# Score stores on ScalarE's queue, a later second batch and later value loads in a fused attention and expert kernel

## The chip, the cores and the metric

The kernel runs on one core of a Trainium2 chip. A core has five engines that work at the same time, each through its own instructions in order: TensorE (PE in the profile, with its weight loads as PEld), VectorE (DVE), ScalarE (ACT), GpSimd (POOL) and SyncE (SP). They meet at semaphores. Transfers between the chip's main memory (HBM) and the core's own memory (SBUF) are made by 16 DMA engines; an engine's instruction only starts one. Matrix products land in a small memory of eight banks (PSUM).

The metric is the device time of one execution in microseconds, lower being better.

## The reference

Eight batches of talking-heads attention with 12 heads, 448 positions and 64 dimensions a head, followed by a gated feed-forward network on all 3584 tokens:

```python
scores = scale * np.matmul(q, k.transpose(0, 1, 3, 2))
scores = np.einsum('bhij,hg->bgij', scores, w_pre)
scores = scores - np.max(scores, axis=-1, keepdims=True)
attn = np.exp(scores)
attn = attn / (np.sum(attn, axis=-1, keepdims=True) + 1e-09)
attn = np.einsum('bhij,hg->bgij', attn, w_post)
attn_out = np.matmul(attn, v)
x = attn_out.transpose(0, 2, 1, 3).reshape(B * S, H * D)
out = ((x @ w1) * (x @ w2) @ w3) @ w_out
```

The two einsums mix the twelve heads with each other, one before and one after the softmax. That is why the scores of all heads of a query row must be together before the softmax of that row can begin.

## The kernel before

**Scores and their way through memory.** `qk` (L166) computes one score unit (b, p, c): batch b, head pair p of six, and a block c of 128 query rows (c = 0, 1, 2; the fourth block, c = 3, holds the last 64 rows of two head pairs). It takes two PSUM banks, eight matmuls, and two copies into a tile `st` of 128 x 2 x 448 floats (L179 and L180, both on ACT but for the first block of batch 0). The tile is then stored to `raw_d[b]` in HBM, where a row holds all heads side by side. A unit with c < 3 is one store of 448 KB (L188); one with c = 3 is two of 224 KB (L185). There are 21 units a batch.

`st` has two buffers in each of two pools: units of batch 0 with an odd p use `qp`, all others use `kp`. The first block of batch 0 goes to a tile `sz` of its own; its first 48 rows (FIRST) are stored at once, and the other 80 a little later in one transfer of 1680 KB, called `held` (L805, made at L881).

**The loop.** Everything after the start runs in a loop over n (L889), called steps here. There are 45 tiles of ten query rows in a batch; a pair m of tiles takes two steps. In an even step n = 2m, `fetch(m + 2)` loads the raw scores of a tile pair from HBM into one of two `r` buffers (L202), DVE finds the row minima (`largest`, L227) and ACT the exponentials (`exp`, L235). In an odd step DVE and POOL scale the post-mixing weights (L244 to L247), `post` multiplies them in (L260, PE), ACT copies that out (L274), and `mix(m + 1)` does the pre-mixing of the next pair (L220, PE). A block of 15 tiles is later multiplied with the values (`av`, L301, PE); for batch 0 the first of these products stand at steps 19 and 21.

**Which unit runs in which step** is set by a table `qks` (L809 to L819). Batch 0's units with c = 1, 2 take steps 0 to 11 and those with c = 3 steps 12 to 14. Batch 1's 21 units begin at step 11 and come every 28/21 steps; later batches are spread over 45 steps each. A unit with c = 0 has its queries and keys (`kq`, 448 KB, L157) loaded six steps ahead. Values (`v`, 256 KB, L286) are loaded one per step from step 6 to 11 for batch 0, and one by one after that.

**The order on SP.** Before the change every transfer is issued by SP. A step issues in this order: the fetch, then whatever the step before left in the list `later` (the stores of that step's score units among it), then the remaining `kq` columns of batch 0 or one value load, then the `kq` loads of the table, then one piece of weights (`cs`, L103, 384 KB). So a store is issued in the step after its copies, behind that step's fetch.

**What else runs meanwhile.** The weights come as 64-bit words, and in nearly every step of the opening one piece is converted to float32: ACT squares (L110), DVE puts the bits together (L121 to L124), ACT and POOL split the result in two parts (L129, L130). w3 and w_out are folded into one matrix on PE (L360); from step 18 on this folding is spread over the steps by `shares` (L833) so that PE is evenly full.

Of the kernel before, what the change touches and what calls it, by code (L numbers as in the profile page):

```python
# [17 lines left out]
HP = H // 2  # L18
IB = 10
GI = H * IB  # L20
NB = -(-S // IB)
QT, NJ = 128, 4
# [5 lines left out]
PP = 64  # L28
JB = S // PP
SETS = NB * B // 2  # L30
FIRST = 48
# [19 lines left out]
class Kernel:  # L51
# [114 lines left out]
    def qk(self, b, p, c, banks):  # L166


        nc = self.nc
        ps = [self.bank(i, f"psq{b}_{p}_{c}_{s}")[:, :S] for s, i in enumerate(banks)]  # L170
        for z, (t, q, k) in enumerate(self.parts(b, p, c)):
            for s in range(2):
                rows = slice(s * D, (s + 1) * D)
                nc.tensor.matmul(ps[s][z * PP:(z + 1) * PP], t[rows, q:q + PP], t[rows, k:k + S], start=True, stop=True)  # L174
        if b == c == 0:
            st = self.sz[:, 2 * p:2 * p + 2]
        else:
            st = (self.qp if b == 0 and p % 2 else self.kp).tile([128, 2, S], F32, tag="st", name=f"st{b}_{p}_{c}", bufs=2)
        nc.scalar.copy(st[:, 0], ps[0])  # L179
        (nc.vector.tensor_copy if b == c == 0 else nc.scalar.copy)(st[:, 1], ps[1])  # L180
        raw = self.raw_d[b]
        if c == 3:
            def store():
                for z in range(2):
                    nc.sync.dma_start(raw[3 * QT:, 2 * (p + z) - 2:2 * (p + z)], st[z * PP:(z + 1) * PP])  # L185
            return store
        n = QT if b or c else FIRST
        return lambda: nc.sync.dma_start(raw[c * QT:c * QT + n, 2 * p:2 * p + 2], st[:n])  # L188

# [549 lines left out]
    def run(self):  # L741
        nc, tc = self.nc, self.tc
# [52 lines left out]
        held = []  # L795
# [6 lines left out]
        next(fold_pieces)  # L802
        for f in held:
            f()
        held = lambda: nc.sync.dma_start(self.raw_d[0][FIRST:QT], self.sz[FIRST:])  # L805

# [1 line left out]
        for n, u in enumerate([(0, p, c) for c in (1, 2) for p in range(HP)] + [(0, p, 3) for p in range(1, HP, 2)]):  # L810
            qks[n] = [u]
        for b in range(1, B):
            first, per = (11, 28 / 21) if b == 1 else ((b - 1) * NB - 6, NB / 21)
            units = [(b, p, c) for g in range(0, HP, 2) for p, c in [*itertools.product((g, g + 1), range(3)), (g + 1, 3)]]
            for i, (b, p, c) in enumerate(units):
                n = int(first + i * per) | (b > 1)
                qks.setdefault(n, []).append((b, p, c))
                if c == 0:
                    loads.setdefault(max(n - 6, 0), []).append((b, p))  # L819
        for b in range(B):  # L820
            for a in range(NG):
                for g in range(HP):
                    n = (b * NB + (a + 1) * GB + 3) | 1
# [25 lines left out]
        for pair in range(ONE // 2, B // 2 - 1):  # L849
            first = P_AT if pair == ONE // 2 else 2 * NB * (pair + 1) + 13  # L850
# [5 lines left out]
        def advance(count):  # L856
            nonlocal done
            for _ in range(min(count, total - done)):
                next(background)
                done += 1  # L860
                self.age += len(self.ends) > 0
                if self.age > 2:
                    self.do_ends()

        def there(p):

            f, r = divmod(p - 3 - 2 * KF, 3)
            return 2 * KF * 3 * (1 + f) + (0, 9, 18)[r] if f >= 0 else min(max(3 * (p - 3), 0), KF * 3)
# [3 lines left out]
        def others(p):  # L872
            nc.sync.dma_start(self.kqs[0, p][:, QT + S:], self.kq0[p][:, QT + S:])
# [4 lines left out]
            self.fetch(m)  # L878
        next(fold_pieces)
        next(fold_pieces)  # L880
        held()  # L881
        next(fold_pieces)
        next(fold_pieces)
        self.mix(0)
# [4 lines left out]
        for n in range(N + 6):  # L889
            self.step, third = n, False  # L890
            if n == GB + 1:
                self.close("qp")
                self.xp = [self.pool("xp0", 1)]
            if n == SWITCH:
                assert done == total
                next(background, None)
                self.do_ends()
                self.do_soon()
                self.do_later()
                assert not fold_pieces  # L900
                self.close("fp")
                self.wp = self.pool("wp", 5, side="right")
                self.up = self.pool("up", 1, side="right")
                self.xp.append(self.pool("xp1", 1, side="right"))
                background, total, done = self.experts(phases), (E_1 + E_2) * ONE + P_1 * (B - ONE) // 2, 0
            if n == LATE:
                assert done >= E_1
                self.close("xp0", "cx")
                self.xq, self.cb = self.pool("xq", 2), self.pool("cb", 1)
            if n == PAIR:  # L910

                assert done >= 2 * E_1 + E_2 and unit_pieces is None and not self.jobs and not self.ys
                self.do_ends()
                self.do_soon()
                self.do_later()
                self.pairs, self.w_ahead = True, 4
                self.close("xp1", "cb", "xq", "cs")
                self.xq = self.pool("xq", 2)
                self.up2 = self.pool("up2", 1, side="right")
                self.free += range(N_UP, NS)  # L920
                setup = self.pair_setup(phases)
            if PAIR <= n < PAIR + 7:
                next(setup, None)
            m, odd = divmod(n, 2)
            if not odd and LF <= n + LF < N:
                self.fetch(m + LF // 2)
            self.do_later()
            if n + 3 < HP:
                others(n + 3)
            elif HP <= n < 2 * HP:  # L930
                self.load_v()
            for x in loads.get(n, []):
                self.load_kq(*x)

            p, pieces = self.n_made - 1 if fold_pieces else 2 * KF + 3 * KF, None
            if avs.get(n):
                pass
            elif fold_pieces:
                f = (self.n_made - 1 - 2 * KF) // 3
                if f < 2 or done >= 2 * KF * 3 * (f - 1):  # L940
                    pieces = fold_pieces
                    if next(pieces, self) is self:
                        fold_pieces = pieces = None
            if m < SETS:
                if odd:
                    self.scale(m)
                else:
                    self.largest(m)
            self.do_soon()
            if pieces:  # L950
                next(pieces)
            elif unit_pieces and not fold_pieces and not avs.get(n):
                ahead = 1 if n < SWITCH else 2 * done // (3 * K1) + 4 + (done > 0)
                if n_pieces < ahead:
                    n_pieces += 1
                    if next(unit_pieces, self) is self:
                        unit_pieces = None
                    else:
                        next(unit_pieces)
                        third = True  # L960
            now = share.get(n, 0)
            if n < SWITCH:

                wanted += now
                now = max(min(there(p), KF * 3 + wanted) - done, 0)
            self.do_sums()

            advance(now // 2)
            self.do_ends()
            if not odd and m < SETS:  # L970
                self.exp(m)
            advance(now - now // 2)
            for x in avs.get(n, []):
                self.av(*x)
            self.do_ends()
            if odd and 1 <= m <= SETS:
                self.post(m - 1)
            if odd and m + 1 < SETS:
                self.mix(m + 1)
            self.do_ends()  # L980
            for i, x in enumerate(qks.get(n, [])):
                self.later.append(self.qk(*x, (6, 7) if i else (0, 1)))
            if third:
                next(unit_pieces)

# [66 lines left out]
```

## Time and profile before

| | |
|---|---|
| median of 3 runs | 1444.0 us (1441.49 to 1446.57) |
| the profiled execution | 1437.83 us |
| its span, first to last instruction | 1436.1 us |
| mean granted TensorE clock | 0.986 |
| PE busy | 1382.4 us, 96% of the span |
| ACT busy | 832.4 us, 58% |
| DVE busy | 741.1 us, 52% |
| moved by the DMA engines | 416.87 MB, mean 290 GB/s |

All of it goes through one hardware queue, SP's:

```profile
q1 hardware_dynamic: 203552, 413.94, 87.6%
```

The columns are packets, megabytes, and the share of the 16 DMA engines' span that the packets took. Times within the profile are of the profiled execution, in microseconds from its start. In the views, `out<-in` names what an instruction writes and reads, `xN` counts merged instructions, and brackets at the end of a row of the timeline give how long the engine was idle before it and what ended that wait. A DMA row on SP (SPq) is only the issue; the data lands later.

### The profile page before, as it was taken

What the parts mean: (1) busy time and instruction counts of PE and PEld (TensorE: products, weight loads), DVE (VectorE), ACT (ScalarE), POOL (GpSimd) and SP (SyncE); (2) the same over time, 40 slices, a digit from 0 to 9 for tenths busy, and PEclk for the clock granted to TensorE, in tenths of its full rate; (3) what the DMA queues carried; (4) which work ended last, traced back from release to release, by engine and by line L of the source; (5) the groups of instructions that cost most, each with busy time, mean ns of one, the idle gap of its engine ahead of it and who ended that gap; (6) DMA issues with size and microseconds to landing.
All of it is one profiled execution on the core that took longest, in us unless ns stands there. A gap on an engine that the chain in (4) does not pass through costs nothing.

```text
span 1436.1 us, 45775 instructions
## 1 busy us (share of the span) xinstructions
PE 1382.4 (96%) x18684; PEld 1055.2 (73%) x18684; DVE 741.1 (52%) x1497; ACT 832.4 (58%) x1952; POOL 620.3 (43%) x754
## 2 busy tenths in 40 slices
PE   5889999999999999999999999999999999999998
PEld 2457786776677667776777777777777777899988
DVE  6867566767544544432444436334444446345563
ACT  4867666777766666665656556556555445422231
POOL 2433233434433544532345336334335446446693
PEclk7989999999999999999999999999999999999999
DMA  8998789999999999999989979799879757698775
GB/s 294 366 326 279 236 270 322 320 312 317 324 286 348 355 356 330 362 346 349 287 275 290 320 259 280 249 323 354 288 229 281 241 177 223 195 337 270 231 232 171
DMA packets 203761, 416.87 MB, mean 290 GB/s; under 512 B 20528, under 2 KB 120112, under 8 KB 203472
## 3 DMA queue, kind: packets, MB, share of 16 engines
q1 hardware_dynamic: 203552, 413.94, 87.6%
q8 instruction: 149, 2.44, 0.7%
q14 instruction: 60, 0.49, 0.1%
HBM read 279.77 MB, written 134.09 MB: 288 GB/s over the span
## 4 chain that ended last, share of the span: by engine, by line
PE 82%; DMA 8%; DVE 4%; ACT 2%; issue 1%; POOL 1%; SPq 0%; DVEq 0%; POOLq 0%; ACTq 0%
PE e L702 21%; PE psa L301 11%; PE pso L260 10%; PE psm L220 9%; PE psq L174 7%; PE eg L522 5%; PE psf L360 4%; PE eo L553 4%; PE e2o L702 4%; PE e1o L702 4%; PE e3o L702 4%; DMA wu<-w_d 3%; DMA r<-raw_d 2%; DMA raw_d<-st 2%; ACT e L235 1%
## 5 line engine op out<-in xcount | busy, mean ns | idle before, releaser
L247 POOL TENSOR_SCALAR w<-wpo,ri 128x60 f32<-128x60 f32 x360 | 180.7, 518 | 485.1 <-DVE ri L245 465.3
L227 DVE TENSOR_REDUCE mn<-psm 128x1 f32<-128x448 f32 x360 | 207.7, 618 | 321.6 <-PE psm L220 321.3
L274 ACT COPY mt<-pso 128x480 f32<-128x480 f32 x352 | 197.9, 621 | 185.8 <-PE pso L260 185.6
L702 PE MATMUL e<-eh,wu 128*128 128x448 f32 x1008 | 296.8, 371 | 6.4 <-DVE c L656 3.2
L235 ACT ACTIVATE e<-psm,mn 128x448 f32<-128x448 f32 x360 | 226.8, 643 | 7.9 <-DVE mn L227 7.9
L702 PEld LDWEIGHTS e<-eh,wu 128*128 128x128 f32 x1008 | 187.5, 188 | 52.2 <-issue 26.8
L260 PEld LDWEIGHTS pso<-w,e 60*64 60x64 f32 x10080 | 175.2, 135 | 51.0 <-issue 42.5
L220 PE MATMUL psm<-r,wsc 60*64 60x448 f32 (+1 forms) x1440 | 191.2, 550 | 19.1 <-DVE cx L124 8.3
L260 PE MATMUL pso<-w,e 60*64 60x60 f32 x10080 | 199.1, 224 | 0.4 <-ACT mt L274 0.3
L702 PE MATMUL e<-el,wu 128*128 128x448 f32 x504 | 186.9, 371 | 0.0
L301 PE MATMUL psa<-mt,v 128*64 128x150 f32 (+1 forms) x2304 | 156.9, 292 | 4.1 <-ACT st L179 4.1
L301 PEld LDWEIGHTS psa<-mt,v 128*64 128x64 f32 x2304 | 143.6, 137 | 20.1 <-ACT st L179 6.7
L174 PE MATMUL psq<-kq 64*64 64x448 f32 x1176 | 154.6, 542 | 2.4 <-ACT st L179 2.4
L656 DVE TENSOR_TENSOR c<-c,e 128x448 f32<-128x448 f32 x168 | 101.7, 618 | 87.7 <-PE e L702 82.9
L179 ACT COPY st<-psq 128x448 f32<-128x448 f32 x162 | 86.4, 533 | 73.7 <-ACT mt L274 34.1
L522 PE MATMUL eg<-xh,wu 128*128 128x448 f32 x384 | 119.2, 381 | 6.3 <-DMA wu<-w_d 6.3
L641 POOL TENSOR_TENSOR el<-x,eh 128x448 fp32r<-128x448 f32 x90 | 103.7, 1170 | 32.8 <-ACT eh L640 29.9
L702 PEld LDWEIGHTS e<-el,wu 128*128 128x128 f32 x504 | 94.6, 188 | 22.5 <-issue 14.1
L174 PEld LDWEIGHTS psq<-kq 64*64 64x64 f32 x1176 | 60.8, 135 | 56.4 <-issue 28.8
L522 PEld LDWEIGHTS eg<-xh,wu 128*128 128x128 f32 x384 | 71.9, 190 | 38.7 <-issue 24.0
L244 DVE TENSOR_SCALAR sa<-sm 128x2 f32<-128x2 f32 x180 | 34.9, 194 | 113.6 <-ACT e L235 113.1
L180 ACT COPY st<-psq 128x448 f32<-128x448 f32 x162 | 87.6, 541 | 0.0
(99 smaller groups left out, 2010.1 us busy)
## 6 DMA issues: line engine op xcount, KB each, us to landing
r<-raw_d SPq DMA_DIRECT2D x344, 210.0 KB, 5.1
raw_d<-st SPq DMA_DIRECT2D x138, 448.0 KB, 6.1
wu<-w_d SPq DMA_DIRECT2D x104, 384.0 KB, 6.7
wu<-s_d SPq DMA_DIRECT2D x96, 384.0 KB, 4.8
wu<-w_d SPq DMA_DIRECT2D x51, 512.0 KB, 5.5
kq<-kq SPq DMA_DIRECT2D x42, 448.0 KB, 7.0
wu<-s_d SPq DMA_DIRECT2D x36, 512.0 KB, 4.9
x<-x_d SPq DMA_DIRECT2D x72, 224.0 KB, 5.7
```

The lines of the kernel that those rows point to most:

```text
L174: nc.tensor.matmul(ps[s][z * PP:(z + 1) * PP], t[rows, q:q + PP], t[rows, k:k + S], start=True, stop=True)
L220: nc.tensor.matmul(ps[s][c * PP:(c + 1) * PP, :S], self.wsc[k], r[k, c], start=True, stop=True)
L227: self.nc.vector.tensor_reduce(mn[:, s:s + 1], self.psm[m][s][:, :S], axis=AX.X, op=ALU.min)
L235: nc.scalar.activation(e, p[:, :S], AF.Exp, bias=mn[:, s:s + 1], scale=-1.0, accum_out=sm[:, s:s + 1])
L247: nc.gpsimd.tensor_scalar_mul(w2[:, s], self.wpo, ri[:, s:s + 1])
L260: nc.tensor.matmul(self.pso[c][z * PP:(z + 1) * PP, at:at + HK], e[k, j * PP:(j + 1) * PP], w2s[k, s], start=True, stop=True)
L274: self.nc.scalar.copy(dst.rearrange("p j g (s i) -> p j s g i", s=2), src)
L301: nc.tensor.matmul(self.psa[rows, g % 3, :W], v[:, j, rows], mt[:, j, 2 * g + s, :W], start=(j == 0), stop=(j == NJ - 1))
L522: nc.tensor.matmul(p, u[:, k % (K1 // 2), x], xs[y][:, k], start=(k == 0 and t == 0), stop=(k == K1 - 1 and t == 2))
L641: nc.gpsimd.tensor_tensor(lo, x, hi.bitcast(F32), op=ALU.subtract)
L656: nc.vector.tensor_tensor(a[out], a[to[0]], p, op=ALU.add)
L702: nc.tensor.matmul(p, w[:, k, x], ops[m, k][y], start=(k == 0 and t == 0), stop=(k == nk - 1 and t == 2))
```

## The change

It has four parts.

1. Score stores of batches 0 and 1 are issued by ACT (`nc.scalar.dma_start`) and no longer by SP, but for the first 48 rows of batch 0's first block, which stay with SP. They are issued in the step of the unit, right behind its copies, and not through `later`. Stores of batches 2 to 7 stay as they were.
2. The held store of rows 48 to 127 becomes two, rows 48 to 63 and 64 to 127, on ACT, at the same place of the program.
3. Batch 1's units begin at step 14 and come every 1.2 steps. Its `kq` loads move with them, being tied to six steps ahead.
4. The first six value loads come at steps 11 to 16 and no longer at 6 to 11.

```diff
-        raw = self.raw_d[b]
-        if c == 3:
-            def store():
+        raw, dma = self.raw_d[b], nc.sync.dma_start if b > 1 or b == c == 0 else nc.scalar.dma_start
+
+        def store():
+            if c == 3:
                 for z in range(2):
-                    nc.sync.dma_start(raw[3 * QT:, 2 * (p + z) - 2:2 * (p + z)], st[z * PP:(z + 1) * PP])
-            return store
-        n = QT if b or c else FIRST
-        return lambda: nc.sync.dma_start(raw[c * QT:c * QT + n, 2 * p:2 * p + 2], st[:n])
+                    dma(raw[3 * QT:, 2 * (p + z) - 2:2 * (p + z)], st[z * PP:(z + 1) * PP])
+            else:
+                n = QT if b or c else FIRST
+                dma(raw[c * QT:c * QT + n, 2 * p:2 * p + 2], st[:n])
+
+        return store
...
-        held = lambda: nc.sync.dma_start(self.raw_d[0][FIRST:QT], self.sz[FIRST:])
+        held = [lambda k=k: nc.scalar.dma_start(self.raw_d[0][k], self.sz[k]) for k in (slice(FIRST, PP), slice(PP, QT))]
...
-            first, per = (11, 28 / 21) if b == 1 else ((b - 1) * NB - 6, NB / 21)
+            first, per = (14, 1.2) if b == 1 else ((b - 1) * NB - 6, NB / 21)
...
-        held()
+        for f in held:
+            f()
...
-            elif HP <= n < 2 * HP:
+            elif HP <= n - 5 < 2 * HP:
                 self.load_v()
...
-                self.later.append(self.qk(*x, (6, 7) if i else (0, 1)))
+                store = self.qk(*x, (6, 7) if i else (0, 1))
+                if x[0] > 1:
+                    self.later.append(store)
+                else:
+                    store()
```

## The prediction

> **What bounds the kernel now.** First the top of the page and its row of slices, to see where the matrix engine is not full.
>
> ```profile
> span 1436.1 us, 45775 instructions
> PE 1382.4 (96%) x18684; PEld 1055.2 (73%) x18684; DVE 741.1 (52%) x1497; ACT 832.4 (58%) x1952; POOL 620.3 (43%) x754
> ...
> PE   5889999999999999999999999999999999999998
> ...
> DMA  8998789999999999999989979799879757698775
> ```
>
> PE is busy 1382.4 of 1436.1 us. A slice is 36 us, and only the first three of PE's row (5, 8, 8) are below nine tenths before the last slice. The change acts on batches 0 and 1, so it must win or lose in these slices, the opening. The busy time by stretches shows what fills them (columns: stretch, length, busy of PE, PEld, DVE, ACT, POOL, granted clock, DMA share, GB/s).
>
> ```profile
> 14.00:20.00 6.00, 1.84 (x9) 0.93 (x13) 3.81 (x6) 1.25 (x3) 2.30 (x3) 0.50 0.77 199
> ...
> 28.00:55.00 27.00, 23.73 (x347) 11.74 (x344) 25.33 (x50) 23.04 (x55) 10.87 (x14) 0.89 1.02 352
> 55.00:66.00 11.00, 9.12 (x111) 4.84 (x111) 10.43 (x20) 9.74 (x24) 5.10 (x8) 0.84 1.02 360
> 66.00:82.00 16.00, 10.05 (x137) 4.89 (x131) 7.69 (x14) 8.79 (x22) 4.05 (x5) 0.68 1.04 378
> 82.00:98.00 16.00, 13.23 (x166) 8.76 (x162) 12.56 (x25) 11.49 (x29) 6.59 (x8) 0.90 0.96 336
> 98.00:112.00 14.00, 13.36 (x241) 9.91 (x237) 6.74 (x15) 8.27 (x20) 2.95 (x6) 1.00 0.68 215
> 112.00:200.00 88.00, 87.36 (x1190) 68.66 (x1187) 62.36 (x127) 61.23 (x148) 28.42 (x40) 1.00 0.87 275
> ```
>
> From 28 to 55 us (steps 1 to 8) DVE is busy 25.33 of 27 us and sets the pace, ACT is close behind with 23.04, and the DMA engines are full. From 55 to 98 us (steps 9 to 18) the DMA engines are still full, but now PE, DVE and ACT all stand: from 66 to 82 us DVE works 7.69 of 16 us. From 112 us on PE is full (87.36 of 88) and whatever is added to PE adds time. What the engines wait for in the bad stretch is in ACT's waits from 55 to 98 us, and one of PE's waits from 18 to 100 us:
>
> ```profile
> ACT st L179 <- DMA raw_d<-st: 8.8, 4, 4.1
> ACT st L179 <- PE psm L220: 2.9, 1, 2.9
> ```
>
> ```profile
> PE psm L220 <- DMA r<-raw_d: 1.6, 1, 1.6
> ```
>
> ACT works in order, and four times it stands before copying a score tile because both buffers of that tile are still being stored: 8.8 us. Why the stores are so late shows in SP's queue from 42 to 51 us, with two of SP's waits from 42 to 55 us, and the store's own durations from 28 to 98 us:
>
> ```profile
> 42.60 0.33 SPq L157 DMA_DIRECT2D kq<-kq  x1
> 43.63 0.33 SPq L103 DMA_DIRECT2D cs<-wo  x1
> 45.01 1.00 SPq L202 DMA_DIRECT2D r<-raw_d  x2
> 46.66 0.35 SPq L188 DMA_DIRECT2D raw_d<-st  x1
> 47.21 0.36 SPq L286 DMA_DIRECT2D v<-v  x1
> 48.20 0.33 SPq L103 DMA_DIRECT2D cs<-wo  x1
> 49.32 0.33 SPq L188 DMA_DIRECT2D raw_d<-st  x1
> 50.73 0.33 SPq L286 DMA_DIRECT2D v<-v  x1
> ```
>
> ```profile
> SPq L202 <- DMA raw_d<-st: 2.0, 1, 2.0
> ...
> SPq L286 <- DMA kq<-kq: 1.1, 1, 1.1
> ```
>
> ```profile
> L188 SPq DMA_DIRECT2D raw_d<-st x18: 325/348/497, 28.8 to 96.7; - x18
> ...
> DMA to landing us min/median/max: 6.2/7.5/8.1
> ```
>
> The value load (L286) writes a fresh buffer, so it needs nothing; yet it waits 1.1 us for the landing of the kq load issued at 42.60. Between them stand eight transfers (kq, cs, two r, st, v, cs, st). So SP keeps about eight in flight, and issues the next when the oldest lands. Each store therefore waits its turn among loads, and behind a fetch (L202) that itself waited 2.0 us for an earlier store. A store takes 0.348 us to issue and 7.5 to land. How late that makes the stores, in the timeline, and two pieces of the chain of work that ended last:
>
> ```profile
> 59.82 0.57 ACT L180 COPY st<-psq 128x448 f32<-128x448 f32 x1
> ...
> 63.30 0.56 ACT L180 COPY st<-psq 128x448 f32<-128x448 f32 x1
> ...
> 66.84 0.33 SPq L188 DMA_DIRECT2D raw_d<-st  x1
> ...
> 74.11 0.53 ACT L179 COPY st<-psq 128x448 f32<-128x448 f32 x1 [2.69 <-DMA raw_d<-st]
> ```
>
> ```profile
> 71.09 7.26 DMA raw_d<-st
> ...
> 87.56 8.09 DMA raw_d<-st
> ```
>
> The tile of step 10 is ready at 59.82 + 0.57 = 60.4 and its store is issued at 66.84, 6.4 us later; step 11's is ready at 63.9 and issued at 71.09, 7.2 us later. ACT's wait that ends at 74.11 is for the first of them, and the one after the second lands (71.09 + 7.26 = 78.4) is 1.5 us. The fourth (87.56 + 8.09 = 95.7, 4.1 us) is a store that was hardly late: there the landing itself is too long.
>
> **The change, part by part.** *Stores on ACT's queue.* 44 transfers leave SP: 12 tiles and 3 x 2 halves of batch 0, 18 and 3 x 2 of batch 1, and the held store of rows 48 to 127 as two. Each is now issued by ACT right behind its copies. Step 10's goes at 60.5 and lands by 68.0 even at 7.5 us, before the 74.11 - 2.69 = 71.4 at which ACT first asks; step 11's goes at 64 and lands by 71.5, before 76.9. These waits go, and the first small one: 8.8 - 4.1 = 4.7 us. Of the fourth I take half, 2.0 (between 0.9, the lateness of that store, and 4.1). With stores out of SP's eight places a fetch is issued earlier, so PE's 1.6 us wait for r goes too. Engine time to be won from 55 to 98 us: 4.7 + 2.0 + 1.6 = 8.3 us.
>
> *The price on ACT.* No row shows ACT issuing a transfer. The nearest is SP's 0.348 us; ACT must also let its last copy finish. I take 0.42, with 0.33 below and 1.35 above (the longest store issue on SP in the whole run); halves cost more:
>
> ```profile
> L188 SPq DMA_DIRECT2D raw_d<-st x138: 320/343/1352, 28.8 to 1071.5; - x138
> L185 SPq DMA_DIRECT2D raw_d<-st x48: 451/578/1519, 74.1 to 1079.5; - x48
> ```
>
> From 28 to 55 us come 8 stores, 3.4 us, into 27 - 23.04 = 4.0 us of ACT's idle time; since ACT and DVE wait for each other I let 1.0 us show (0 to 3.4). From 55 to 98 us ACT idles 43 - 30.0 = 13.0 us, of which 4.7 + 2.0 go; 6.3 remain for 8 stores at 0.42 and 6 halves at 0.65, 7.3 us: 1.0 us shows. Behind an issuing ACT stand the cast of the next weight piece (L129), which POOL waits for, and the exponentials, which the next mix on PE waits for. So the engines can win 8.3 - 2.0 = 6.3 us.
>
> *Batch 1 starts at step 14, every 1.2 steps.* Before, its units fall on 11, 12, 13, 15, 16, 17, 19, 20 and on; after, on 14 to 18, 20 and on. Steps 11 to 13 no longer hold two units. Up to step 19 there are 7 before and 5 after: two stores of 448 KB, 0.92 MB, leave the full stretch, 2.5 us at 0.36 MB/us. The kq loads, six steps ahead of each first unit, go from 5, 9, 14, 18 to 8, 11, 16, 20, each still six steps early. The two units are not saved: they now run where PE is full, at 0.75 us each in the chain there:
>
> ```profile
> 190.29 0.75 PE psq L174 x8
> ```
>
> That is +1.5 us. The last unit moves from step 37 to 38; batch 1's first fetch is at step 40, so nothing is late.
>
> *Values five steps later.* Six loads of 256 KB go from steps 6 to 11 to steps 11 to 16. The products at steps 19 and 21 want them, three or more steps later, while landing takes 7.5 us, two steps. That costs nothing; it thins the stretch before 55 us and thickens the one behind it.
>
> *Is there room on the DMA engines?* They are full to 98 us, so 6.3 us of engine time can only be had if bytes leave. 2.5 us leave with the two units, and from 98 to 112 us the share is 0.68: 14 x 0.32 = 4.5 us stand idle, into which prefetches can slide. 2.5 + 4.5 = 7.0 is just above 6.3, so the engines decide, narrowly.
>
> The Trainium skill ("DMA: Bandwidth & Descriptors", "Issuing engines are not separate DMA queues") speaks against that: transfers from all issuers run on the same 16 engines, and a second issuer saves only issue time. The share of 1.02 fits it, and by it the sum would be that of the first rival below. The same page ("Queues, rings and completion order") says each DMA engine takes turns between queues by packets; a store alone in its queue would then land sooner than 7.5 us and a load later, and the fourth wait would go whole, 2.1 us more. No row of this trace shows two busy queues.
>
> *The held store.* SP issues it at 17.18; on ACT it stands behind the second square of the conversion, which ends at 13.9:
>
> ```profile
> 13.32 0.57 ACT L110 ACTIVATE cm<-cs 128x384 f32<-128x384 f32 x1
> ...
> 17.18 0.42 SPq L805 DMA_DIRECT2D raw_d<-sz  x1
> ```
>
> ```profile
> 17.65 10.36 DMA cs<-wo
> ```
>
> The weight load behind it is on the chain for 10.36 us. From 14 to 20 us the DMA share is 0.77, so 6 x 0.23 = 1.4 us of DMA time can be used that stood idle: -1.4 us (between +1, if the first r loads, which then share with it, come late, and -3.3, the head start).
>
> *Behind 98 us.* ACT is 61.23 of 88 us busy there and takes 18 units' stores more; PE waits for ACT now and then, and I add 0.5 us (0 to 2).
>
> **The sum**: -6.3 - 1.4 + 1.5 + 0.5 = -5.7 us, against the profiled execution's 1437.83 us (span 1436.1 and 1.7 around it): 1432.1. The three timed runs have a median of 1444.0, 6.2 above that execution; on their scale the forecast is 1444.0 - 5.7 = 1438.3, or 1438.5.
>
> **The rivals.** *Bytes decide.* If prefetches don't slide into the slack behind 98 us, the stretch gives only its 2.5 us: -2.5 - 1.4 + 2.0 = -1.9, 1442. For it: a share of 1.02 to 1.04 with no gap in 54 us. Against: most of these bytes are loaded up to five pieces ahead and need not have landed by 98 us. Chance 0.24.
>
> *More than forecast.* If the fourth wait goes whole and the clock, 0.68 from 66 to 82 us, stays near 0.9, another 4 us go: about -10, 1434. For it: PE is slow there just because it stands. Against: ACT and the DMA engines are full. Chance 0.12.
>
> *ACT becomes the bound (slower).* In steps 1 to 18 there are 22 issues of p us each. If only half of ACT's 4.0 + 6.3 us of idle time can be used, 22p - 5.2 shows; gains are 8.3 + 1.4 and later costs 2.0. It breaks even at p = 0.58 and is 0.3% slower at 0.78; at 0.85 it is +5.8, 1450. For it: halves take 0.58 and full queues up to 1.35. Against: the median of stores in the full stretch is 0.348. Chance 0.14.
>
> *Loads starve.* Stores beside them make r land after its three steps of lead: five fetches from step 12 to 20 at the 1.6 us seen once, +8.0: +2.3, 1446.5. Chance 0.08. *It does nothing*, because stores still wait for the same places as SP's: then bytes alone remain, and it is counted with the first.
>
> **Chances and range.** A measurement of this kernel can tell about 0.3%, 4.3 us, from no change. The forecast (1435.5 to 1440.5) has 0.42, of which 0.08 lies within 0.3%; with 0.12 of the larger gain and 0.02 of the first rival that is 0.48 faster. Within 0.3%: 0.08 + 0.22 + half of the starving = 0.34. Slower: 0.14 + 0.04 = 0.18. The range 1431 to 1448 leaves out most of the slow case and the end of the fast one.
>
> **What would show it.** Right: ACT's waits for raw_d<-st nearly gone before 100 us; ACT issues near 0.4 us; step 19's first product (L301) several us before 96.3; the two units back in PE's full stretch. Wrong: ACT over 95% busy or issuing from 28 to 98 us with DVE waiting for it; r or weight waits in place of store waits; or the same 98 us with stores landing early and everything else late.

## The result and the profile after

The changed kernel is slower: 1452.78 us median (1451.71 to 1453.6, 4 runs) against 1444.77 us (1441.49 to 1446.57, 4 runs) of the kernel before beside it. The ratio is 1.0059, 95% interval 1.0041 to 1.0076, or about +8 us. Forecast were 1438.5 us and a range up to 1448.

The top of the page of the changed kernel, and the rows of its DMA queues (packets, megabytes, share of the engines' span):

```profile
span 1451.8 us, 45729 instructions
...
PE   4779999999999999999999999999999999999998
...
q1 hardware_dynamic: 198176, 395.70, 83.6%
q10 hardware_dynamic: 5392, 18.24, 3.6%
```

18.24 MB have moved to ACT's queue (q10), as meant. But the first three slices of PE are 4, 7, 7 where they were 5, 8, 8: the opening, where time was to be won, has become emptier. The busy time by the same stretches as in the prediction:

```profile
14.00:20.00 6.00, 0.00 (x0) 0.00 (x0) 3.72 (x6) 1.25 (x3) 2.21 (x3) 0.50 1.08 266
...
28.00:55.00 27.00, 23.29 (x284) 10.42 (x277) 25.48 (x49) 22.09 (x53) 12.07 (x15) 0.89 1.03 348
55.00:66.00 11.00, 6.93 (x148) 3.83 (x147) 9.37 (x18) 6.39 (x16) 3.17 (x4) 1.00 0.95 310
66.00:82.00 16.00, 10.29 (x110) 4.43 (x114) 12.09 (x24) 11.85 (x28) 6.02 (x8) 0.88 1.04 365
82.00:98.00 16.00, 12.05 (x169) 7.78 (x162) 10.96 (x21) 12.42 (x30) 6.05 (x8) 0.80 0.99 324
```

From 14 to 20 us PE does nothing at all (1.84 us before), and from 55 to 66 us ACT is busy 6.39 us (9.74 before). The bad stretch from 66 to 82 us is better, as forecast: DVE 12.09 us against 7.69, though the changed kernel runs some 4 us behind by then and the stretches do not hold quite the same steps. ACT's waits from 20 to 112 us, and then one of PE's up to 100 us, say what came in place of the old ones:

```profile
ACT cm L110 <- DMA cs<-wo: 10.1, 1, 10.1
ACT fo L129 <- DMA cs<-wo: 3.9, 1, 3.9
...
ACT st L179 <- DMA raw_d<-st: 0.3, 1, 0.3
```

```profile
PE psm L223 <- DMA r<-raw_d: 15.2, 1, 15.2
```

The waits at the same two places in the kernel before, ACT's and then PE's:

```profile
ACT cm L110 <- DMA cs<-wo: 6.5, 2, 4.5
```

```profile
PE psm L220 <- DVE cx L124: 8.3, 1, 8.3
```

The store waits did go, from 8.8 us to 0.3. In their place PE waits 15.2 us and not 8.3 before its first mix, ACT waits 10.1 us and not 6.5 for weights, and there is a new stand of 3.9 us at a cast (L129).

**Where the time is lost, step by step.** Each even step has two row minima on DVE (L227 before, L230 after). The start of the first one is a clock for the step; the difference to the same step of the kernel before is the lag. First before, at steps 22 and 46, then after:

```profile
111.55 0.62 DVE L227 TENSOR_REDUCE mn<-psm 128x1 f32<-128x448 f32 x1 [0.56 <-PE psm L220]
...
204.62 0.62 DVE L227 TENSOR_REDUCE mn<-psm 128x1 f32<-128x448 f32 x1 [1.23 <-PE psm L220]
```

```profile
116.08 0.62 DVE L230 TENSOR_REDUCE mn<-psm 128x1 f32<-128x448 f32 x1 [0.56 <-PE psm L223]
...
213.18 0.62 DVE L230 TENSOR_REDUCE mn<-psm 128x1 f32<-128x448 f32 x1 [2.92 <-PE psm L223]
```

So 4.5 us are lost by step 22 and 4.1 more between 22 and 46, 8.6 in all. From there to step 130 the lag stays between 8.6 and 9.0. Later it grows to 15.8 in these two profiles, but the profiled execution of the kernel before (1437.83 us) lies 7 us under its median. The lags are therefore read up to step 46, and the whole by the timed ratios. Two of the kernels below, held_on_sync and act_a_step_later, turned out to be nearly the same program; their lags differ by up to 1.5 us, so a single lag is not good to less. The lags of all kernels, in us against the kernel before:

| kernel | step 0 | 4 | 8 | 12 | 18 | 22 | 46 | timed ratio (95%) |
|---|---|---|---|---|---|---|---|---|
| after | 6.9 | 3.9 | 4.3 | 7.5 | 4.9 | 4.5 | 8.6 | 1.0059 (1.0041 to 1.0076) |
| held_on_sync | 0.1 | 3.6 | 5.3 | 6.2 | 4.9 | 4.5 | 8.6 | 1.0066 (1.0043 to 1.009) |
| only_held_act | 7.6 | 4.6 | 4.6 | 4.6 | 2.3 | 3.5 | 3.6 | 1.001 (0.9991 to 1.003) |
| held_sync_early | 7.1 | 4.1 | 4.1 | 4.1 | 2.0 | 0.5 | 0.6 | one run, 1449.11 us |
| only_stores_act | 0.1 | 4.3 | 5.6 | 11.2 | 9.6 | 8.8 | 8.8 | 1.0058 (1.0041 to 1.0074) |
| act_a_step_later | 0.0 | 4.2 | 5.1 | 7.3 | 5.9 | 6.0 | 10.1 | 1.0112 (1.0079 to 1.0145) |
| first_two_on_sync | -0.1 | 2.5 | 3.6 | 5.7 | 6.0 | 8.6 | 12.7 | one run, 1462.21 us |
| sync_at_once | 0.2 | 0.9 | 1.2 | 1.2 | -3.6 | 1.9 | 5.9 | 1.005 (1.0027 to 1.0073) |
| only_units_late | 0.2 | 1.1 | 1.1 | 1.1 | 0.6 | 1.8 | 6.1 | 1.0075 (1.0054 to 1.0096) |
| units_17 | 0.1 | 0.5 | 0.9 | 0.9 | -1.0 | -1.8 | 3.6 | one run, 1450.94 us |
| only_values_late | 0.2 | 1.4 | 1.6 | 1.6 | -2.6 | -0.4 | -0.4 | 1.0024 (1.0009 to 1.0038) |
| values_late_units_dense | -0.3 | 0.5 | 0.5 | 0.5 | 1.3 | 3.2 | 3.1 | one run, 1445.55 us |
| in_step_on_sync | -0.2 | 0.0 | 0.2 | 0.2 | -4.4 | -2.0 | -2.0 | 0.9983 (0.9969 to 0.9997) |

### The profile page after: what moved, and what is told of

Same layout as the page of the kernel before. It is cut to its first block, busy times and chain, and to the rows that moved or that the text cites. A ratio compares the mean times of both kernels' runs of the same rounds, so it can differ in the third digit from the quotient of the medians.

```text
span 1451.8 us, 45729 instructions
## 1 busy us (share of the span) xinstructions
PE 1385.4 (95%) x18684; PEld 1054.7 (73%) x18684; DVE 739.4 (51%) x1497; ACT 833.9 (57%) x1952; POOL 617.7 (43%) x754
## 3 DMA queue, kind: packets, MB, share of 16 engines
q10 hardware_dynamic: 5392, 18.24, 3.6%
## 4 chain that ended last, share of the span: by engine, by line
PE 77%; DMA 12%; DVE 4%; ACT 4%; issue 2%; POOL 1%; SPq 1%; ACTq 0%; DVEq 0%; POOLq 0%
PE e L705 20%; PE psa L304 10%; PE pso L263 10%; PE psm L223 8%; PE psq L174 7%; PE eg L525 5%; PE psf L363 4%; PE eo L556 4%; DMA wu<-w_d 4%; PE e2o L705 4%; PE e3o L705 4%; PE e1o L705 2%; DMA x<-x_d 2%; DMA raw_d<-st 2%; DMA r<-raw_d 2%
## 5 line engine op out<-in xcount | busy, mean ns | idle before, releaser
L230 DVE TENSOR_REDUCE mn<-psm 128x1 f32<-128x448 f32 x360 | 207.7, 618 | 342.6 <-PE psm L223 342.6
L180 ACT COPY st<-psq 128x448 f32<-128x448 f32 x162 | 87.7, 541 | 0.0
```

The lines of the kernel that those rows point to most:

```text
L230: self.nc.vector.tensor_reduce(mn[:, s:s + 1], self.psm[m][s][:, :S], axis=AX.X, op=ALU.min)
```

## Experiments

**The held store: undone, and alone.** Undone (held_on_sync):

```diff
-        held = [lambda k=k: nc.scalar.dma_start(self.raw_d[0][k], self.sz[k]) for k in (slice(FIRST, PP), slice(PP, QT))]
+        held = [lambda: nc.sync.dma_start(self.raw_d[0][FIRST:QT], self.sz[FIRST:])]
```

> The changed kernel with one part undone: the held store of rows 48 to 127 is again one transfer on SP, behind the first r loads. Theory A (the early held store on ACT's queue starves the first r and weight loads): the first row minimum, at 27.7 us in the changed kernel and 20.8 before, comes back to about 21 us, the second from 33.9 to about 30.5, and the whole run is 3 to 4 us shorter than the changed kernel: ratio to before 1.003. Theory B (the loss is ACT's issuing and the two units moved behind step 20): the start may come back but the whole stays within 1 us of the changed kernel, ratio 1.006.

> The kernel before with this part alone: the held store as two on ACT's queue. Theory A: first row minimum near 27.7 us, second near 33.9, and 3 to 4 us lost at step 2; the later store waits of before can eat or keep that; ratio to before 1.0025. Theory B: below 1.001.

The start came back (step 0 at +0.1), but by step 22 the lag was again 4.5 us and the ratio 1.0066. Alone (only_held_act, the same line of the diff the other way, in the kernel before) it delays step 0 by 7.6 us, keeps 4.6 to step 12 and 3.6 at step 46; the ratio of 1.001 is unclear. So the early held store delays the start by itself, how much of that reaches the whole is not shown, and in the changed kernel the delay is hidden, because something else holds step 22 just as late. Theory A fell as the cause of the whole.

What the store does at the start shows in ACT's and then SP's timeline of the changed kernel:

```profile
12.97 0.35 ACTq L808 DMA_DIRECT2D raw_d<-sz  x1
...
14.07 0.49 ACTq L808 DMA_DIRECT2D raw_d<-sz  x1
```

```profile
15.07 6.23 SPq L205 DMA_DIRECT2D r<-raw_d  x4
```

The four r loads right behind it take 6.23 us to issue (1.74 before, at 14.95), and PE's first mix starts at 25 us in place of 18. Is that the second queue, or only 1680 KB put ahead of r? held_sync_early leaves the store on SP and moves the call up, ahead of the fetches:

```diff
+        held()
         for m in range(LF // 2):
             self.fetch(m)
...
-        held()
```

> The kernel before with the held store still on SP as one transfer, but ahead of the first r loads. If the start loses because 1.68 MB go ahead of r and the weights, whoever issues them, the row minimum of step 0 comes 4 to 7 us late as with the store on ACT (7.6). If it loses because a second queue is favoured over SP's, step 0 is less than 2 us late, since r then waits only its turn behind a store that started earlier.

Step 0 came 7.1 us late, nearly the same as on ACT's queue. In SP's timeline, and in a wait of PE up to 100 us:

```profile
14.65 0.43 SPq L805 DMA_DIRECT2D raw_d<-sz  x1
15.77 6.61 SPq L202 DMA_DIRECT2D r<-raw_d  x4
```

```profile
PE psm L220 <- DMA r<-raw_d: 14.8, 1, 14.8
```

It is the order, not the queue, that costs the start: the large store goes ahead of the loads that PE wants first. It is no dependency either, since in the compiled programs of both kernels none of the four loads waits for that store. At step 22 the store on SP is only 0.5 us late, the one on ACT 3.5; that difference was not followed.

**The stores on ACT, alone.** only_stores_act leaves held store, units and values as before:

```diff
-        raw = self.raw_d[b]
+        raw, dma = self.raw_d[b], nc.sync.dma_start if b > 1 or b == c == 0 else nc.scalar.dma_start
...
+                if x[0] > 1:
+                    self.later.append(store)
+                else:
+                    store()
```

> The kernel before with this part alone: the score stores of batches 0 and 1 on ACT, right behind their copies; held store, units and values as before. My prediction's step (late stores on SP cost 4.7 us and more): ACT's waits for stores nearly gone and ratio 0.996 to 0.998. Theory B (issuing on ACT costs what the waits gave): ratio 1.000 to 1.003, with weight loads or r late in place of the stores.

It loses as much as the whole change: 8.8 us at step 46, ratio 1.0058, more than either theory gave it. In held_on_sync the loss begins at step 1, in ACT's timeline:

```profile
30.20 0.54 ACT L180 COPY st<-psq 128x448 f32<-128x448 f32 x1
...
34.26 0.33 ACTq L189 DMA_DIRECT2D raw_d<-st  x1
34.63 0.51 ACT L129 CAST fo<-cx 128x384 fp32r<-128x384 f32 x1 [3.90 <-DMA cs<-wo]
```

The copy ends at 30.74, the store is issued at 34.26: ACT stands 3.5 us in between, and the cast behind it is put down as waiting for a cs load that it does not need. The compiled program of this kernel says what the two wait for:

```
L189 DMA raw0_d_62<-st0_1_1_324 128x896 [waits DMAHW0_49,Activation_49]
L129 CAST fo_148<-cx4_307 128x384 [waits DVE_49]
```

The cast waits for DVE alone. The store waits for ACT's own copies and for DMAHW0. There are eight such semaphores (DMAHW0 to 7; a semaphore is a counter that one instruction raises and another waits for). Transfers of *both* queues carry them in turn, and each waits until the transfer that had its semaphore before has landed. For this store that is a cs load issued by SP, the very load that the profile names beside the cast. So a store on ACT waits for an older transfer, mostly one of SP's (30 of the 44 that ACT issues in the changed kernel), and ACT computes nothing meanwhile. The changed kernel has the same at step 9, and PE's next mix then waits for the exponentials that come behind it on ACT:

```profile
61.65 0.58 ACT L180 COPY st<-psq 128x448 f32<-128x448 f32 x1
...
65.76 0.33 ACTq L189 DMA_DIRECT2D raw_d<-st  x1
66.12 0.51 ACT L129 CAST fo<-cx 128x384 fp32r<-128x384 f32 x1 [3.90 <-DMA cs<-wo]
```

```profile
67.75 1.64 PE L223 MATMUL psm<-r,wsc 60*64 60x448 f32 x5 [3.64 <-ACT e L238]
```

The changed kernel's lag is 4.6 us at step 10 and 7.5 at step 12. In only_stores_act the three longest stands, 3.8, 2.1 and 2.6 us (between the end of an L180 copy and the issue behind it), fall at steps 1, 7 and 9, and its lag grows from 1.8 to 4.3 between steps 2 and 4, from 5.6 to 7.8 between 8 and 10, and to 11.2 at step 12.

**Who waits, or what moves?** Stores that come sooner also take the DMA engines from weights and r. Two runs were meant to take ACT's stand away, and neither did:

```diff
-... if b > 1 or b == c == 0 else nc.scalar.dma_start
+... if b > 1 or b == c == 0 or (b == 0 and c == 1 and p < 2) else nc.scalar.dma_start
```

> The changed kernel with the held store on SP and, besides, the stores of steps 0 and 1 on SP, at the same place of the program. With the held store on SP alone, ACT stands 3.5 us at the store of step 1 (issued at 34.26) for the landing of an older transfer, and the row minimum of step 4 is 3.6 us later than before. Theory C (a store on ACT must wait until one of eight earlier transfers, SP's among them, has landed, and ACT computes nothing meanwhile): with SP waiting in its place step 4 is less than 1 us late, and step 8, 5.3 late there, 1 to 2.5 late. Theory D (the loads are late because the stores share the DMA engines with them, whoever issues them): step 4 stays 3 us late or more.

With steps 0 and 1 on SP step 4 is 2.5 us late, between the two expectations: the stand moved to the next store on ACT, that of step 2, which waits 3.6 us. Step 22 is 8.6 us late.

```diff
-                if x[0] > 1:
-                    self.later.append(store)
-                else:
-                    store()
+                self.later.append(store)
```

> The changed kernel with the held store on SP and the score stores still on ACT, but issued in the next step, as the kernel before does on SP. Theory C: the older transfers have mostly landed by then, ACT's stand of 3.5 us at step 1's store shrinks below 1 us, step 8 is 1 to 3 us late and no more 5.3, and the whole is 1 to 3 us shorter than with the store right behind the copies, though the 4 us between steps 22 and 46 stay: ratio 1.002 to 1.005. Theory D: no gain, ratio 1.006.

A stand of 4.2 us remained in the opening, step 8 was 5.1 us late and the ratio 1.0112. But this edit does not do what was meant. A step ends with the unit's copies and the next begins with the stores of `later`, and ACT has nothing to do in between. So in the compiled program each store still stands right behind its copies on ACT, and all transfers have the order and the semaphores of held_on_sync; only in step 14 two copies come ahead of two stores. ACT's timeline shows it at the first store:

```profile
24.66 0.55 ACT L180 COPY st<-psq 128x448 f32<-128x448 f32 x1
25.24 0.35 ACTq L189 DMA_DIRECT2D raw_d<-st  x1
```

Whether a store that ACT issues later would cost less is therefore not tested. The run is held_on_sync over again, and shows how far apart two such measurements can lie: 1.0112 and 1.0066, 10.1 and 8.6 us at step 46.

The third run speaks to the question itself. sync_at_once is held_on_sync with one line changed, all stores on SP but still issued in the unit's own step:

```diff
-        raw, dma = self.raw_d[b], nc.sync.dma_start if b > 1 or b == c == 0 else nc.scalar.dma_start
+        raw, dma = self.raw_d[b], nc.sync.dma_start
```

> The changed kernel with held store and score stores all back on SP, but the score stores still issued in the unit's own step, at the same place of the program as on ACT. Bytes and order of the program are those of the changed kernel with the held store on SP; only the engine that waits for the older transfers differs. Theory C (ACT standing at its stores is the cost): ACT's stands of 3.5 and 2.5 us are gone, the row minimum of step 8 is at most 1.5 us late (5.3 there) and step 12 at most 2 (6.2). Theory D (the stores take the DMA engines from weights and r, whoever issues them): steps 8 and 12 stay 4 to 6 us late. Both: 4 us more are lost between steps 22 and 46 through the units.

Step 8 is 1.2 us late and not 5.3, step 12 1.2 and not 6.2. ACT's timeline at the same place:

```profile
29.83 0.54 ACT L180 COPY st<-psq 128x448 f32<-128x448 f32 x1
31.22 0.51 ACT L129 CAST fo<-cx 128x384 fp32r<-128x384 f32 x1 [0.86 <-DVE cx L124]
```

The cast follows after 0.86 us. What the stand does to DVE shows at the next weight piece, first in held_on_sync, then in sync_at_once:

```profile
35.62 1.01 DVE L124 SCALAR_TENSOR_TENSOR cx<-cm,cx 128x384 f32<-128x384 f32 x1 [1.48 <-ACT cm L110]
```

```profile
34.32 0.56 DVE L124 SCALAR_TENSOR_TENSOR cx<-cm,cx 128x384 f32<-128x384 f32 x1
```

The same units are stored, but now SP waits. Theory D, by which steps 8 and 12 stay 4 to 6 us late, fell, and ACT's standing is seen where the lag grows. One reserve remains. The two programs also differ in order: SP issues the store of step 0 at 29.21, behind the fetch of step 2, where ACT issued it at 25.54, ahead of that fetch, and the older transfer that a store is paired with differs too. How much of the 4 to 5 us saved comes from that was not taken apart.

**The units.** Alone, in the kernel before, and once more with twice the number behind step 22:

```diff
-            first, per = (11, 28 / 21) if b == 1 else ((b - 1) * NB - 6, NB / 21)
+            first, per = (14, 1.2) if b == 1 else ((b - 1) * NB - 6, NB / 21)
```

> The kernel before with this part alone: batch 1's units from step 14, every 1.2 steps. If two units moved behind step 20 cost what PE shows: 1.5 to 2 us lost between steps 22 and 46, and up to 2.5 us won before step 20 by bytes that leave: ratio 0.999 to 1.001. If the loss of 4.1 us that the changed kernel shows between steps 22 and 46 is all from the units: ratio 1.001 to 1.003.

> The kernel before with batch 1's units from step 17, one a step. From step 22 on there are 16 of them, against 12 before and 14 with the start at 14. If each unit moved behind step 22 costs about 2.1 us of PE's full stretch (4.4 for two), the lag between steps 22 and 46 grows by 8.5 us; if by my figure of 0.75 us each, by 3 us; if the loss has to do with the start at 14 as such and not with their number, by about 4.

From step 14 (only_units_late) the lag grows by 4.4 us between steps 22 and 46, from 17 on (units_17, `(17, 1.0)`) by 5.4. All six kernels with the start at step 14 lose 4.0 to 4.4 us there, and none with the units of before more than 0.2, so the units are the cause. Alone they cost a ratio of 1.0075, above both expectations and no less than the whole change. PE's busy time on the scores (psq) and on the weight folding (psf) between steps 22 and 46, first before, then after (the first figure behind the length is PE's):

```profile
111.55:204.62 93.07, 15.70 (x132) 5.57 (x128) 0.00 (x0) 15.49 (x32) 1.00 0.87 275
...
111.55:204.62 93.07, 52.98 (x281) 48.18 (x281) 6.10 (x11) 5.82 (x12) 1.00 0.87 275
```

```profile
116.08:213.18 97.10, 17.64 (x148) 5.34 (x144) 0.00 (x0) 17.42 (x36) 1.00 0.83 268
...
116.08:213.18 97.10, 54.34 (x282) 48.26 (x282) 6.09 (x11) 5.76 (x12) 1.00 0.83 268
```

Two units, 16 matmuls, add 1.94 us, 0.97 each. In units_17 psq takes 19.64 us for four units more, 0.98 each. The folding takes 1.36 us longer for one matmul more, and the rest of the 4.0 us is mostly idle time. In units_17 the lag grows by only 1 us for the two further units. So a unit costs 1 us of PE there, and what is left, 2.1 us in the changed kernel, 2.4 in only_units_late and 1.4 in units_17, does not grow with their number; that it comes from the new order is an inference. Why the folding matmuls run longer was not tested.

The win before step 22 came and went: only_units_late starts step 14 4.1 us early (72.81 against 76.91), step 16 0.5 us late and step 22 1.8. The store waits grow, probably because units in five successive steps share two buffers. ACT's wait from 20 to 112 us in only_units_late (8.8 us before), and the longest one in the timeline:

```profile
ACT st L179 <- DMA raw_d<-st: 12.0, 5, 6.3
```

```profile
79.19 0.53 ACT L179 COPY st<-psq 128x448 f32<-128x448 f32 x1 [6.34 <-DMA raw_d<-st]
```

**The values, and a version of the parts that cost nothing.**

```diff
-            elif HP <= n < 2 * HP:
+            elif HP <= n - 5 < 2 * HP:
```

> The kernel before with the first six value loads at steps 11 to 16. My prediction put nothing on it. If the DMA engines decide the steps up to 20, the steps up to 10 come no earlier (they are held by DVE and ACT) and steps 12 to 18 come later, since 1.5 MB arrive where batch 1's units and the halves already are: 0 to 4 us late at step 18, ratio 1.000 to 1.003. If it takes load off the stretch: 0 to 3 us earlier.

> The kernel before with values at steps 11 to 16 and batch 1's units from step 11 every 1.2 steps: 11 units behind step 22 against 12 before. If units behind step 22 cost about 1 us each in PE's full stretch and the order the rest, the stretch from step 22 to 46 is 0 to 2 us shorter than before's 93.1; whether that survives depends on how late step 22 is by the bytes that come forward, 0 to 5 us.

Values alone (only_values_late) make step 18 2.6 us earlier and step 46 0.4. The timed ratio is still 1.0024: the loss comes behind step 60 and was not followed. With batch 1's units from step 11 every 1.2 steps besides, the stretch from 22 to 46 is 0.1 us shorter, but step 22 is 3.2 us late.

in_step_on_sync is sync_at_once without the new units:

```diff
-            elif HP <= n < 2 * HP:
+            elif HP <= n - 5 < 2 * HP:
...
-                self.later.append(self.qk(*x, (6, 7) if i else (0, 1)))
+                store = self.qk(*x, (6, 7) if i else (0, 1))
+                if x[0] > 1:
+                    self.later.append(store)
+                else:
+                    store()
```

> The kernel before with values at steps 11 to 16 and the score stores of batches 0 and 1 on SP but issued in their own step; units and held store as before. It keeps the parts of the change that cost nothing alone. If a store issued in its own step is worth what my prediction said (4.7 us of ACT's waits), step 22 is 2 to 5 us earlier than before and stays so, since the units behind it are those of before: ratio 0.997 to 0.999. If the waits only move to the next store, because the DMA engines are full up to step 19, step 22 is within 1 us and the ratio within 0.999 to 1.002.

1441.09 us median against 1445.17 (10 and 13 runs), ratio 0.9983 (0.9969 to 0.9997): a little faster than the kernel before, with an interval that ends just below 1. Step 18 is 4.4 us early, step 22 still 2.0, and that stays to step 130. ACT's store waits from 20 to 112 us are nearly as long as before:

```profile
ACT st L179 <- DMA raw_d<-st: 7.0, 3, 4.8
```

**The ladder.** Four rungs lead from the kernel before to the changed one; the first adds two parts, the others one each. The lags at step 46:

| from | to | what is added | lag at step 46 |
|---|---|---|---|
| before | in_step_on_sync | values late, stores in their own step on SP | -2.0 |
| in_step_on_sync | sync_at_once | units from step 14 | +7.9 |
| sync_at_once | held_on_sync | score stores on ACT | +2.7 |
| held_on_sync | after | held store on ACT | 0.0 |

The sum is 8.6 us. The order matters: stores on ACT cost 8.8 us by themselves, with the earlier values and units, and 2.7 as the third rung, most likely because the units have already made step 22 late. As a single lag is only good to some 1.5 us, the 2.7 is rough.

## Why the prediction was wrong, point by point

- **What bounds the kernel** held in the main. The whole loss of about 8 us stands at step 46: 4.5 us of it arise in the opening, and 4.1 behind it, where PE is full and added work adds time.
- **Stores late on SP, eight places**: the reading of eight transfers in flight was right, and the store waits went (8.8 to 0.3 us). The step that failed is "with stores out of SP's eight places". They are not SP's: ACT's transfers take the same eight, so nothing left the row, and the wait moved from SP, which has nothing else to do, to ACT, which does. Where the sum had 6.3 us won, the stores on ACT alone lost 8.8 by step 46. The remark under the rivals that stores could still "wait for the same places as SP's" had the mechanism, but it put the price at nothing. The stores did land a little sooner, 6.7 us at the median from 28 to 98 us against 7.5; that did not help, and step 19's first product, forecast several us before 96.3, started at 101.4.
- **The price on ACT** was taken as the issue alone, and the issue itself was sized about right. In the changed kernel, over the whole run:

```profile
L189 ACTq DMA_DIRECT2D raw_d<-st x30: 321/326/389, 31.3 to 181.3; - x30
L186 ACTq DMA_DIRECT2D raw_d<-st x12: 452/534/923, 76.7 to 189.6; - x12
```

  0.326 and 0.534 us stand against 0.42 and 0.65. The term left out is the wait ahead of the issue, up to 3.5 us in the changed kernel and 3.8 in only_stores_act. The rival "ACT becomes the bound" had the right engine and place, but worked with the price per issue.
- **Two units behind step 20** were put at +1.5 us and measured 4.1 between steps 22 and 46: 0.97 each and not 0.75, and 2.1 more, a term the sum did not have and whose cause stays open.
- **2.5 us won by bytes that leave** did not last: alone, the units made step 14 4.1 us earlier and step 22 1.8 later. The store waits, taken to end with the lateness on SP, stayed at 7.0 us in in_step_on_sync, whose stores are issued sooner, and grew to 12.0 in only_units_late.
- **The held store** was put at -1.4 us, +1 at worst. It costs 6.9 us at step 0 and 3.7 at step 2. The head start was counted, the r loads behind it were not worked out. By step 22 it is hidden (4.53 us late with it, 4.51 without).
- **Behind 98 us** 0.5 us was added for ACT's issues. only_stores_act loses nothing between steps 22 and 46, 8.8 us late at both.
- **The values** at nothing: right up to step 46 (-0.4). Over the whole run they cost a ratio of 1.0024 alone, and why is open.
- **The Trainium skill's rule** that a second issuing queue saves only issue time ("DMA: Bandwidth & Descriptors", "Issuing engines are not separate DMA queues") was the first rival's. That no time came from the second queue, with a ratio of 1.0058 for the stores alone, fits it. That ACT lost time by waiting for SP's transfers goes beyond it.

## What to carry to other kernels

A transfer issued by a computing engine costs that engine every wait of the transfer, so read in the compiled program what it waits for, completion semaphores shared with other queues included, before moving it off SP. Work moved from a stretch that waits into one where PE is full costs its matmuls and what it does to the order of the others: here 2 us for the matmuls and 2 more that were not explained. When several edits are made at once, build a ladder that adds one part at a time and compare the start of each step: losses that hide each other (here the held store's) show, and parts that are worth keeping, too.

## What the runs showed that was not expected

- 1680 KB stored just ahead of four 210 KB loads make their issue take 6.2 to 6.6 us, not 1.7, and their first user wait 15 us, not 8.3, with the store on either queue (as one transfer on SP, as two on ACT).
- ACT issues a 448 KB store in 0.326 us (median), slightly less than SP with 0.343.
- A cast was put down as waiting 3.9 us for a load that it does not use: the wait was that of the transfer issue ahead of it on its engine, which has no row of its own in ACT's waits.
- Behind step 60 the lags of these kernels move by up to 11 us more, mostly upward, against a profiled execution of the kernel before that itself lies 7 us under its median, though the change touches nothing there. It was not found what sets them, and the timed ratios hold them: only_units_late is 6.1 us late at step 46 and 10.8 (1.0075) in all.
